# First stage of a long convolution on quarters of TensorE's array: even and odd positions apart, their sums and differences by VectorE and GpSimd

## The chip, the cores and the metric

One core of a Trainium2 chip runs the whole kernel. The metric is the device time of one execution in microseconds; the median of the runs shown counts. The engines are TensorE (PE; its weight loads are shown as PEld), VectorE (DVE), ScalarE (ACT), GpSimd (POOL) and SyncE (SP), which issues the DMAs here. TensorE multiplies a stationary operand by a moving one into PSUM; the other engines work between PSUM and SBUF, except that GpSimd works in SBUF alone.

## What is computed

The input is x, 8 sequences of 6400 positions and 128 channels in fp32, and a filter h of 6400 positions and 128 channels. Each channel is convolved with its filter (causally, by Fourier transforms), and then goes through a gated projection:

```python
Yf = np.fft.rfft(x, n=2*S, axis=1) * np.fft.rfft(h, n=2*S, axis=0)[None]
y = np.fft.irfft(Yf, n=2*S, axis=1)[:, :S, :]
gate = sigmoid(sum(conv_w[k] * shifted(y, 4 - k) for k in range(5)))
out = (gate * (y @ w_val)) @ w_out
```

## The kernel before

**The transform.** A sequence of 6400 positions is seen as 100 x 64. For each channel the transform is made in four stages, all matmuls in fp32:

- First stage (`first_stage`): over the 100. The stationary operand is one channel's 100 x 64 block of x, the moving one 100 columns of the constant `r1_sb` (cosines, or minus the sines), so that the real part lands in PSUM's partitions 0 to 63 and the imaginary part in 64 to 127. A group is 8 channels, 16 matmuls in the code, and fills a place of two PSUM banks. It is then copied into `gy` (the filter's into `dt`) by two copies of 400 elements a partition, both by ScalarE or both by VectorE (`ev`). A sequence has 16 groups.
- Second stage (`second`, 13 blocks of 8 of the 100 frequencies): over the 64, with the constant m2 from memory as stationary operand; then the product with the filter's spectrum (`product`: three long VectorE operations, a copy by ScalarE or GpSimd) and a sum (`summed`) by GpSimd, or for the last MANY blocks by either GpSimd or VectorE; the very last always by VectorE.
- Third stage (`third`): over the 64 back, in two pieces of 512 columns a block, copied out and stored to memory (`zd`).
- Fourth stage (in `longconv_moe`, "chunk"): read back from `zd`, over the 100 back; then five taps for the gate (ScalarE, VectorE, and for tap 3 GpSimd's addition of what ScalarE scaled), the sigmoid, the two projections, the multiplication and the store (`gated`).

**Halves of the array.** Every product of the kernel uses 64 columns of the stationary operand at a time, and two such halves work side by side on different output partitions (`product_of`; in the first stage the real and the imaginary part). In the profile a matmul of the code is two MATMUL and two LDWEIGHTS records, and the 64 columns stand as "*64" in the shape.

**The order.** Nothing is ordered by hand. `_Plan` takes every step with its costs on the engines that may do it (`_pe`, `_act`, `_dve`, `_pool`, `_dma`: formulas in ns written in the code), its predecessors, its PSUM place and its buffers. `due` gives each step a due time from the constants at the top of the file (HEADS, PERIOD, FIRST, SECOND, FOURTH, GATE and so on), `forward` plays the run through and gives each free engine the ready step that is due first. The resulting order is written into the program, and each engine then works through its queue in that order. The fourth stage of one sequence is so woven into the first and second stage of the next.

**Buffers.** PSUM has two places of two banks for the first and second stage (a third one only until the fourth stage begins) and places of one bank for the others. Groups of x are loaded (256 KB each) into buffers that come free when the group's matmuls are done; in steady state there are four. Thirteen buffers k serve the second and third stage. GpSimd steps marked `port` wait, by an added dependency, for the last VectorE step that is marked so.

**Where the profile puts it.** Every operation goes through one helper, so nearly all rows carry L124; the tiles tell them apart. First stage: `ps<-r_sb,x` (or `m_sb`, `y_all`, where the first loads of x lie in buffers that are free at the start). Second: `ps<-gy`. Third: `pb<-k,r_sb`. Fourth: `pb<-m_sb,dt`. Projections: `pb<-y_all,w_sb` and `pb<-dt,w_sb`.

The diff touches lines 31 to 73 (constants), `_constants` (85), `_Op` (163), `_Plan.forward` (236), `longconv_moe` (409) with `first_stage` (551), and `_lay_x` (998).

Of the kernel before, what the change touches and what calls it, by code (L numbers as in the profile page):

```python
# [30 lines left out]
CHUNKS = [HEAD] + [(a, CH) for a in range(0, 60, CH)]  # L31
NCH = len(CHUNKS)
OUT_ORDER = CHUNKS[1:] + [HEAD]
SECOND_END = 44851
FOURTH_END = 7729
GATE_END = 16494
EARLY_END = 14954
QTAPS = (3,)
LAST_QTAPS = (3,)
QB = 2  # L40
# [4 lines left out]
SLOTS = 13  # L45
SPARE = 2
RING = 4
MANY = 2
XB = 4
YB = 6  # L50
HEADS = 46300
HEAD_STEP = 5159
HEAD_END = 112668
PERIOD = 108461
WEIGHTS = 26000
M4 = 60000
ROWS = 50000
FIRST = 1583
SECOND_AT = 44851
SECOND = 4057  # L60
EARLY = 14954
FOURTH = 7729
GATE = 16494
PATIENCE = 380
ROUSE = 3
LASTQ = 10
FIRST3 = 0
LAST3 = 1
SWAPPED = ()
LAST = 3444  # L70
LAST_GATE = 12987
LAST_EARLY = 9555
LAST_LAG = 10


def _out_range(ch):
# [8 lines left out]
def _constants():  # L85
    k1 = np.arange(N1, dtype=np.float64)
    n1 = np.arange(N1, dtype=np.float64)
    k2 = np.arange(N2, dtype=np.float64)
    n2 = np.arange(N2, dtype=np.float64)
    tau = 2.0 * np.pi  # L90
    a = tau * np.outer(n1, k1 + 0.25) / N1
    r1 = np.concatenate([np.cos(a), -np.sin(a)], axis=1)
    al = tau * (
        (k1[None, :, None] + 0.25) * n2[:, None, None] / N
        + np.outer(n2, k2)[:, None, :] / N2
    )
    m2 = np.zeros((2, N2, N1, 2 * N2))
    m2[0, :, :, :N2] = np.cos(al)
    m2[1, :, :, :N2] = np.sin(al)
    m2[0, :, :, N2:] = -np.sin(al)  # L100
    m2[1, :, :, N2:] = np.cos(al)
    b = tau * np.outer(k2, n2) / N2
    r3 = np.zeros((2 * N2, N2, 2))
    r3[:N2, :, 0] = np.cos(b)
    r3[N2:, :, 0] = -np.sin(b)
    r3[:N2, :, 1] = -np.sin(b)
    r3[N2:, :, 1] = -np.cos(b)
    t = N2 * n1[None, :] + n2[:, None]
    g = tau * (k1[:, None, None] + 0.25) * t[None] / N
    m4 = np.zeros((PX, N2 + 1, N1))  # L110
    m4[:N1] = np.concatenate([np.cos(g), np.sin(g[:, :1])], axis=1) / N
    f = lambda v: np.ascontiguousarray(v.astype(np.float32))
    return f(r1), f(m2.reshape(2 * N2, N1, 2 * N2)), f(r3.reshape(2 * N2, 2 * N2)), f(m4.reshape(PX, -1))
# [45 lines left out]
class _Op:  # L159
# [3 lines left out]
    def __init__(self, run, cost, after, bank=None, new=False, port=False, take=None, use=(), wait=(), spare=0):  # L163
        self.run, self.cost, self.bank, self.new, self.port = run, cost, bank, new, port
        self.take, self.use, self.wait, self.spare = take, list(use), [*use, *wait], spare
        for s in [*self.use, *([take] if take else [])]:
            s.users.append(self)
        self.after = [a for a in after if a is not None]
        self.rank = self.at = self.done = self.engine = None


class _Plan:
# [63 lines left out]
    def forward(self):  # L236
# [3 lines left out]
        halves = [[0] * 2 for _ in range(4)]  # L240
        slots = [0] * SLOTS
        self.split = False
        port = server = now = 0
        events, began, lanes = [], [], []
        for o in self.ops:
            o.at = None
# [12 lines left out]
        def fits(o, e):  # L259
            if o.port and e == "vector" and port > now + self.PATIENCE:  # L260
                return False
            if any(max(free[x], now) + c[1] < now + o.cost[e][1] for x, c in o.cost.items() if x != e):
                return False
            if any(s.spot is None for s in o.wait) or o.take is not None and len(open_slots(o)) <= o.spare:
                return False
            b = o.bank
            if b is None:
                return True
            if o.new:
                return all(x.spot is not None for x in b.before) and self.room(b, halves, now) is not None  # L270
            return not any(x != e and t > now for x, t in b.seen)
# [5 lines left out]
        while left:  # L277
            moved = True
            while moved:
                moved = False  # L280
                for e in free:
                    if free[e] > now:
                        continue
                    kept, o = [], None
                    while ready[e]:
                        item = heapq.heappop(ready[e])
                        if item[2].at is not None:
                            continue
                        if fits(item[2], e):
                            o = item[2]  # L290
                            break
                        kept.append(item)
                    for item in kept:
                        heapq.heappush(ready[e], item)
                    if o is None:
                        continue
                    occ, dur = o.cost[e][:2]
                    if o.port and e in ("vector", "gpsimd") and port > now:
                        occ, dur = occ + port - now, dur + port - now
                    o.engine, o.at = e, now  # L300
                    free[e] = now + occ
                    if e == "sync":
                        server = max(now + self.LEAD, server) + dur
                        free[e] = max(free[e], server - self.LEAD - self.AHEAD)
                        o.done = server + self.LAND
                        lanes.append(o.done)
                        free[e] = max(free[e], *lanes[-8:-7], 0)
                    else:
                        o.done = now + dur + self.HOP
                    if o.port and e in ("vector", "gpsimd"):  # L310
                        port = now + dur
                    if o.take is not None:
                        i = o.take.spot = min(open_slots(o), key=lambda i: slots[i])
                        slots[i] = None
                    for s in [*o.use, *([o.take] if o.take else [])]:
                        s.left -= 1
                        if not s.left:
                            slots[s.spot] = max(u.done for u in s.users)
                            heapq.heappush(events, (slots[s.spot], -1, None))
                    b = o.bank  # L320
                    if b is not None:
                        if o.new:
                            i, h = b.spot = self.room(b, halves, now)
                            self.split = self.split or i == 2 and b.n == 1
                            for k in (0, 1) if b.n == 2 or i < 2 else (h,):
                                halves[i][k] = None
                        b.seen.append((e, now + dur + self.HOP))
                        b.left -= 1
                        if not b.left:
                            i, h = b.spot  # L330
                            for k in (0, 1) if b.n == 2 or i < 2 else (h,):
                                halves[i][k] = max(u.done for u in b.users)
                                heapq.heappush(events, (halves[i][k], -1, None))
                    began.append(o)
                    left -= 1
                    heapq.heappush(events, (o.done, self.index[id(o)], o))
                    heapq.heappush(events, (free[e], -1, None))
                    heapq.heappush(events, (now + dur, -1, None))
                    heapq.heappush(events, (now + dur + self.HOP, -1, None))
                    moved = True  # L340
# [68 lines left out]
def longconv_moe(ctx: ExitStack, tc: tile.TileContext, x, h, r1, m2, r3, m4, w64, out):  # L409
# [11 lines left out]
    ga = dt[:, : N2 * N1].rearrange("p (n t) -> p n t", t=N1)  # L421
    z_t = [dt[:, N2 * N1 + i * 2 * CH * C :][:, : 2 * CH * C] for i in range(RING)]
    m4_sb = cp.tile([PX, N2 + 1, N1], F32, name="m4_sb")
    r1_sb = cp.tile([N1, 2 * N1], F32, name="r1_sb")
    r3_sb = cp.tile([128, 2 * N2], F32, name="r3_sb")
    w_sb = cp.tile([C, NW], F32, name="w_sb")
    wc_sb = w_sb[:, 2 * C :]
# [103 lines left out]
    add(rouse, {"tensor": _pe(860, ROUSE)}, [zero], bank=warm, new=True)  # L531
    plan.base = -1500
    loads, firsts, x_at, x_last = [], [], [], {}
    r1_in = dma(r1_sb, r1, 80)
    spare = [m4_sb.rearrange("k n t -> k (n t)")[:, i * XG * N2 : (i + 1) * XG * N2] for i in range(8)]
    spare += y_sb
    x_more = x_sb + [i.rearrange("k (g n) -> k g n", n=N2) for i in spare]
# [1 line left out]
    def load(src):  # L539
# [8 lines left out]
        x_last[i] = n  # L548
        x_at.append(x_more[i])

    def first_stage(src, dst, before, base, step, groups=range(NG)):
        done = []
        for g in groups:
# [3 lines left out]
            load(src[g])  # L557
            t, bank = x_at[n], _Bank(2)

            def mm(e, t=t, bank=bank):  # L560
                for j in range(XG):
                    for c in range(2):
                        nc.tensor.matmul(
                            bank.ap()[c * N2 : (c + 1) * N2, j // 4, (j % 4) * N1 : (j % 4 + 1) * N1],
                            lhsT=t[:N1, j, :],
                            rhs=r1_sb[:, c * N1 : (c + 1) * N1],
                            start=True,
                            stop=True,
# [429 lines left out]
def _lay_x(v):  # L998
    b = v.shape[0]
    q = np.zeros((b, PX, C, N2), np.float32)  # L1000
    q[:, :N1] = v.reshape(b, N1, N2, C).transpose(0, 1, 3, 2)
    q = q.reshape(b, PX, NG, XG, N2).transpose(0, 2, 1, 3, 4)
    return np.ascontiguousarray(q)


def _lay_out(v):
# [33 lines left out]
```

## Time and profile before

| | |
|---|---|
| median of 3 runs | 965.06 us (962.79 to 965.62) |
| the profiled execution | 962.3 us |
| its span | 960.5 us |
| granted TensorE clock | 0.999 |
| TensorE busy | 942.0 us, 98% |
| VectorE busy | 703.7 us, 73% |
| ScalarE busy | 606.5 us, 63% |
| GpSimd busy | 362.7 us, 38% |
| moved by DMA | 283.27 MB, mean 295 GB/s |

All times in the rows below are of the one profiled execution. A row of a group has, after the shapes and the count, the group's busy time in us, the mean of one in ns, and the idle time of the engine ahead of it with what ended it. A row in order of time has the start in us, the length in us, the engine, the operation and the count of records that were merged; its length includes the modelled end of the last matmul. A row of a tile has the shortest, median and longest duration in ns, and the first and last start. The slice of each row of stretches begins with its start and end in us from the beginning of the span.

### The profile page before, as it was taken

To read this page: it belongs to the slowest core of one execution; us is meant where nothing else is said; L and a number is where in the kernel's file an instruction comes from. 1 tells how busy PE (TensorE), PEld (TensorE's weight loads), DVE (VectorE), ACT (ScalarE), POOL (GpSimd) and SP (SyncE) were. 2 spreads that over 40 slices of the span, in tenths; PEclk is the share of its full clock that TensorE was granted. 3 is DMA by queue.
4 is the path that set the end of the run, shared out by engine and by line. 5 is a ranking of instruction groups with operands and counts; after the bars stand their busy time and mean duration, and the time that the engine had idled before them with its cause. 6 is when DMAs were issued, how large, how long until landed. Compare 5 with 4: busy or idle time off the path is not lost.

```text
span 960.5 us, 32555 instructions
## 1 busy us (share of the span) xinstructions
PE 942.0 (98%) x13956; PEld 701.9 (73%) x13956; DVE 703.7 (73%) x855; ACT 606.5 (63%) x1053; POOL 362.7 (38%) x233
## 2 busy tenths in 40 slices
PE   9899999999999999999999999999999999999897
PEld 8888897667966689666876679766886669765553
DVE  2047718996399946998399964999379973999497
ACT  5665666566675657756566666756576666756664
POOL 0045503761047412554046611574026630465230
PEclk9999999999999999999999999999999999999999
DMA  9999798989979997999979898899979999695762
GB/s 349 355 344 323 262 368 284 311 272 342 340 226 325 289 369 263 287 285 329 363 237 320 278 344 320 245 308 309 361 255 297 280 334 333 203 328 180 263 212 105
DMA packets 183902, 283.27 MB, mean 295 GB/s; under 512 B 10538, under 2 KB 128654, under 8 KB 183694
## 3 DMA queue, kind: packets, MB, share of 16 engines
q1 hardware_dynamic: 183758, 281.19, 87.5%
q8 instruction: 110, 1.80, 0.7%
q14 instruction: 34, 0.28, 0.1%
HBM read 195.95 MB, written 88.92 MB: 297 GB/s over the span
## 4 chain that ended last, share of the span: by engine, by line
PE 92%; DVE 5%; issue 2%; POOL 1%; DMA 1%; ACT 0%; DVEq 0%; POOLq 0%
PE pb L124 49%; PE ps L124 43%; DVE dt L124 3%; DVE k L124 1%; POOL dt L124 1%; DMA dt<-zd 1%; ACT dt L124 0%; ACT k L124 0%; ACT q L124 0%; ACT y_head L124 0%; DVE q L124 0%; DVEq L124 0%; POOLq L124 0%
## 5 line engine op out<-in xcount | busy, mean ns | idle before, releaser
L124 DVE SCALAR_TENSOR_TENSOR dt<-pb,w_sb,dt 128x500 f32<-128x500 f32 (+7 forms) x328 | 221.6, 686 | 92.1 <-ACT y_head L124 56.1
L124 POOL TENSOR_TENSOR dt<-dt,q 128x500 f32<-128x500 f32 x93 | 116.6, 1253 | 371.5 <-DVE dt L124 285.8
L124 DVE TENSOR_TENSOR k<-ps,k 64x1024 f32<-64x1024 f32 (+2 forms) x208 | 244.3, 1177 | 5.9 <-issue 3.6
L124 POOL TENSOR_TENSOR k<-k,k 128x1024 f32<-128x1024 f32 x89 | 210.8, 2379 | 93.3 <-DVE k L124 89.8
L124 PEld LDWEIGHTS pb<-m_sb,dt 100*64 100x64 f32 x3976 | 179.5, 137 | 38.4 <-issue 17.4
L124 PE MATMUL pb<-k,r_sb 128*64 128x512 f32 x800 | 192.6, 594 | 0.7 <-DVE dt L124 0.7
L124 PEld LDWEIGHTS ps<-r_sb,x 100*64 100x64 f32 x3776 | 171.0, 137 | 27.1 <-issue 24.5
L124 PE MATMUL pb<-m_sb,dt 100*64 100x100 f32 x3976 | 186.6, 249 | 0.3 <-DVE k L124 0.3
L124 ACT COPY k<-pb 128x512 f32<-128x512 f32 (+1 forms) x207 | 119.0, 580 | 99.6 <-PE pb L124 65.6
L124 PE MATMUL ps<-r_sb,x 100*64 100x100 f32 x3776 | 175.6, 250 | 2.7 <-issue 2.7
L124 ACT COPY gy<-ps 128x400 f32<-128x400 f32 x242 | 114.4, 531 | 79.3 <-PE ps L124 79.3
L124 DVE SCALAR_TENSOR_TENSOR k<-ps,k 64x1024 f32<-64x1024 f32 (+1 forms) x104 | 123.2, 1185 | 55.0 <-PE ps L124 48.7
L124 PEld LDWEIGHTS ps<-gy,k 128*64 128x64 f32 x2176 | 129.3, 135 | 35.9 <-issue 21.3
L124 ACT COPY y_all<-pb 128x500 f32<-128x500 f32 x156 | 89.4, 579 | 93.4 <-PE pb L124 90.5
L124 PE MATMUL ps<-gy,k 128*64 128x128 f32 x2176 | 139.6, 278 | 0.4 <-issue 0.2
L124 PEld LDWEIGHTS pb<-k,r_sb 128*64 128x64 f32 x800 | 56.8, 136 | 80.7 <-issue 52.6
L124 PE MATMUL pb<-dt,w_sb 128*64 128x500 f32 (+2 forms) x412 | 102.4, 574 | 7.0 <-DVE dt L124 6.8
L124 ACT COPY k<-k 64x1024 f32<-64x1024 f32 (+1 forms) x78 | 81.1, 1040 | 17.4 <-DVE k L124 16.2
L124 DVE TENSOR_TENSOR dt<-pb,dt 128x500 f32<-128x500 f32 (+2 forms) x102 | 67.3, 660 | 29.7 <-PE pb L124 16.9
L124 PE MATMUL pb<-y_all,w_sb 128*64 128x500 f32 x336 | 85.1, 588 | 0.0
L124 POOL COPY k<-k 64x1024 f32<-64x1024 f32 (+1 forms) x39 | 36.8, 945 | 104.7 <-ACT k L124 64.9
L124 ACT ACTIVATE dt<-pb,w_sb 128x500 f32<-128x500 f32 (+1 forms) x107 | 68.8, 650 | 7.6 <-PE pb L124 7.5
(53 smaller groups left out, 575.3 us busy)
## 6 DMA issues: line engine op xcount, KB each, us to landing
dt<-zd SPq DMA_DIRECT2D x95, 640.0 KB, 5.6
zd<-k SPq DMA_DIRECT2D x96, 512.0 KB, 4.7
k<-hd SPq DMA_DIRECT2D x84, 512.0 KB, 5.7
k<-m SPq DMA_DIRECT2D x64, 512.0 KB, 5.6
x<-xl SPq DMA_DIRECT2D x110, 256.0 KB, 5.4
out<-y_all SPq DMA_DIRECT2D x84, 250.0 KB, 4.6
hd<-k SPq DMA_DIRECT2D x12, 512.0 KB, 4.5
dt<-zd SPq DMA_DIRECT2D x8, 512.0 KB, 6.6
```

Source lines behind the costliest of these rows:

```text
L124: r = self._tc.keep_in_program_order(call(*args, **kwargs))
```

## The change

From the second sequence on (`QUARTERS = 32` groups: 16 of the filter and 16 of the first sequence stay on the old path) the first stage uses a symmetry of the transform: with the 100 positions split into even and odd ones, frequency k and frequency k + 50 are the sum and the difference of the same two products. So the 50 even positions lie in partitions 0 to 49 and the 50 odd ones in 64 to 113, both in x and in `r1_sb`, and a group is made of 32 matmuls in the code: 50 rows by 64 columns, with 50 moving columns, for each of 8 channels, 2 row halves and 2 column halves. The even products go to one PSUM bank and the odd ones to the other. ScalarE copies both banks (800 elements) to a k buffer, VectorE adds the odd part's copy to the even part in PSUM and writes frequencies 0 to 49 of `gy`, and GpSimd or VectorE writes frequencies 50 to 99 as the difference of the two copies. The filter and the first sequence keep the full contraction, over 128 partitions, in which the new gaps are zeros.

The plan learns of the two shapes: a step has a mode, a change of mode is booked at 95 ns, and while TensorE is in quarters, ready quarter steps that are due within 2175 ns go first. Nearly all due-time constants are new, and MANY goes from 2 to 1 (only the last block's sum is VectorE's). PAIRED is 0, so the lines that it guards do nothing; HALF is 50; BRISK and SLOW are not used.

```diff
-SECOND_END = 44851
-FOURTH_END = 7729
-GATE_END = 16494
-EARLY_END = 14954
+SECOND_END = 42124
+FOURTH_END = 7349
+GATE_END = 16413
+EARLY_END = 13447
...
-MANY = 2
+MANY = 1
...
-HEADS = 46300
-HEAD_STEP = 5159
-HEAD_END = 112668
-PERIOD = 108461
+HEADS = 42326
+HEAD_STEP = 5131
+HEAD_END = 108957
+PERIOD = 101559
...
-FIRST = 1583
-SECOND_AT = 44851
-SECOND = 4057
-EARLY = 14954
-FOURTH = 7729
-GATE = 16494
+FIRST = 2231
+SECOND_AT = 42124
+SECOND = 3721
+EARLY = 13447
+FOURTH = 7349
+GATE = 16413
...
-LAST = 3444
-LAST_GATE = 12987
-LAST_EARLY = 9555
+LAST = 3223
+LAST_GATE = 13546
+LAST_EARLY = 10558
 LAST_LAG = 10
+HALF = 50
+SWITCH = 95
+SAME = 2175
+QUARTERS = 32
...
-    r1 = np.concatenate([np.cos(a), -np.sin(a)], axis=1)
+    w = np.concatenate([np.cos(a), -np.sin(a)], axis=1)
+    r1 = np.zeros((PX, 2 * N1))
+    r1[:HALF], r1[N2 : N2 + HALF] = w[::2], w[1::2]
...
-                    while ready[e]:
+                    if e == "tensor" and mode:
+                        same = [x for x in ready[e] if x[2].mode and x[2].at is None and x[0] < now + SAME and fits(x[2], e)]
+                        if same:
+                            o = min(same)[2]
+                    while ready[e] and o is None:
...
+                    if e == "tensor" and o.mode != mode:
+                        occ, dur, mode = occ + SWITCH, dur + SWITCH, o.mode
...
+    def quarters(g, t, bank, loaded, dst, old):
+        def mm(e, t=t, bank=bank):
+            for j in range(XG):
+                for r in range(2):
+                    for c in range(2):
+                        rows = slice(r * N2, r * N2 + HALF)
+                        nc.tensor.matmul(
+                            bank.ap()[c * N2 : (c + 1) * N2, r, j * HALF : (j + 1) * HALF],
+                            lhsT=t[rows, j, :],
+                            rhs=r1_sb[rows, c * N1 : c * N1 + HALF],
+                            start=True,
+                            stop=True,
+                        )
+        p = add(mm, {"tensor": _pe(118, 8)}, [loaded, r1_in], bank=bank, new=True)
+        p.mode = 1
...
+        kept_ = _Slot()
+        half = lambda v: v.rearrange("p (m t k) -> p m t k", t=2, k=HALF)
+        both = lambda s=kept_: s.ap()[:, : 2 * XG * HALF].rearrange("p (r x) -> p r x", r=2)
+        to = lambda r, g=g: dst(g)[:, :, r * HALF : (r + 1) * HALF].rearrange("p m k t -> p m t k")
+        def out_(e, bank=bank, both=both):
+            nc.scalar.copy(both(), bank.ap()[:, :, : XG * HALF])
+        def plus(e, bank=bank, both=both, to=to, half=half):
+            nc.vector.tensor_tensor(out=to(0), in0=half(bank.ap()[:, 0, : XG * HALF]), in1=half(both()[:, 1]), op=ADD)
+        def minus(e, both=both, to=to, half=half):
+            getattr(nc, e).tensor_tensor(out=to(1), in0=half(both()[:, 0]), in1=half(both()[:, 1]), op=ALU.subtract)
+        o = add(out_, {"scalar": _act(800)}, [p], bank=bank, take=kept_)
+        x = add(plus, {"vector": _dve(400)}, [o, *old], bank=bank, use=[kept_])
+        y = add(minus, {"gpsimd": _pool(400), "vector": _dve(400)}, [o, *old], port=True, use=[kept_])
+        return [x, y]
...
+            if n >= QUARTERS:
+                done += quarters(g, t, bank, loads[n], dst, before(g))
+                continue
...
-                            lhsT=t[:N1, j, :],
+                            lhsT=t[:, j],
...
-    q[:, :N1] = v.reshape(b, N1, N2, C).transpose(0, 1, 3, 2)
+    u = v.reshape(b, N1, N2, C).transpose(0, 1, 3, 2)
+    q[:, :HALF], q[:, N2 : N2 + HALF] = u[:, ::2], u[:, 1::2]
```

More of the change, by code (lines that the diff above doesn't have):

```diff
@@ L69 @@
 SWAPPED = ()
-LAST = 3444
-LAST_GATE = 12987
-LAST_EARLY = 9555
+LAST = 3223
+LAST_GATE = 13546
+LAST_EARLY = 10558
 LAST_LAG = 10
+HALF = 50
+SWITCH = 95
+SAME = 2175
+QUARTERS = 32
+BRISK = 9
+SLOW = 12000
+PAIRED = 0
 def _out_range(ch):
@@ L168, in __init__ @@
         self.after = [a for a in after if a is not None]
-        self.rank = self.at = self.done = self.engine = None
+        self.rank = self.at = self.done = self.engine = self.partner = None
+        self.mode = 0
 class _Plan:
@@ L242, in forward @@
         self.split = False
-        port = server = now = 0
+        port = server = now = mode = 0
         events, began, lanes = [], [], []
@@ L268, in fits @@
                 return True
+            if PAIRED and o.mode and not mode and o.partner is not None and o.partner.at is None:
+                if need[id(o.partner)] or sum(all(t is not None and t <= now for t in p) for p in halves[:3]) < 2:
+                    return False
             if o.new:
@@ L423, in longconv_moe @@
     m4_sb = cp.tile([PX, N2 + 1, N1], F32, name="m4_sb")
-    r1_sb = cp.tile([N1, 2 * N1], F32, name="r1_sb")
+    r1_sb = cp.tile([PX, 2 * N1], F32, name="r1_sb")
     r3_sb = cp.tile([128, 2 * N2], F32, name="r3_sb")
@@ L533, in longconv_moe @@
     loads, firsts, x_at, x_last = [], [], [], {}
-    r1_in = dma(r1_sb, r1, 80)
+    r1_in = dma(r1_sb, r1, 100)
     spare = [m4_sb.rearrange("k n t -> k (n t)")[:, i * XG * N2 : (i + 1) * XG * N2] for i in range(8)]
@@ L549, in load @@
         x_at.append(x_more[i])
+    def quarters(g, t, bank, loaded, dst, old):
[13 more added lines that the diff above has]
+        p.mode = 1
+        p.partner = firsts[-1] if g % 2 else None
+        if g % 2:
+            firsts[-1].partner = p
+        firsts.append(p)
+        kept_ = _Slot()
[12 more added lines that the diff above has]
+        return [x, y]
     def first_stage(src, dst, before, base, step, groups=range(NG)):
@@ L1000, in _lay_x @@
     q = np.zeros((b, PX, C, N2), np.float32)
-    q[:, :N1] = v.reshape(b, N1, N2, C).transpose(0, 1, 3, 2)
-    q = q.reshape(b, PX, NG, XG, N2).transpose(0, 2, 1, 3, 4)
-    return np.ascontiguousarray(q)
+    u = v.reshape(b, N1, N2, C).transpose(0, 1, 3, 2)
+    q[:, :HALF], q[:, N2 : N2 + HALF] = u[:, ::2], u[:, 1::2]
+    return np.ascontiguousarray(q.reshape(b, PX, NG, XG, N2).transpose(0, 2, 1, 3, 4))
 def _lay_out(v):
```

## The prediction

> **What bounds the kernel now.** I read the page first (busy shares and the chain that ended last), then a table of busy time by stretch over one steady sequence, then the matmuls in order of time, and last the durations by form.
>
> ```profile
> span 960.5 us, 32555 instructions
> ...
> PE 942.0 (98%) x13956; PEld 701.9 (73%) x13956; DVE 703.7 (73%) x855; ACT 606.5 (63%) x1053; POOL 362.7 (38%) x233
> ...
> PE 92%; DVE 5%; issue 2%; POOL 1%; DMA 1%; ACT 0%; DVEq 0%; POOLq 0%
> ```
>
> TensorE is busy 98% of the span and makes up 92% of the chain, so TensorE work is worth its full length if nothing else comes up beside it. What could come up is VectorE; the table by stretch says where it has room (columns: length, busy time of PE, PEld, DVE, ACT, POOL with instruction counts, clock, DMA share, GB/s).
>
> ```profile
> 326.00:332.00 6.00, 6.00 (x74) 3.82 (x72) 5.89 (x7) 4.37 (x8) 2.07 (x3) 1.00 1.05 373
> 332.00:338.00 6.00, 6.00 (x70) 3.36 (x68) 5.51 (x10) 4.70 (x9) 1.26 (x1) 1.00 0.95 289
> 338.00:344.00 6.00, 6.00 (x114) 4.92 (x112) 4.04 (x6) 3.75 (x9) 1.56 (x2) 1.00 1.07 358
> 344.00:350.00 6.00, 6.00 (x114) 4.92 (x112) 2.41 (x4) 3.14 (x8) 0.99 (x2) 1.00 1.02 356
> 350.00:356.00 6.00, 6.00 (x104) 4.57 (x100) 1.36 (x2) 3.00 (x7) 0.00 (x0) 1.00 1.03 406
> 356.00:362.00 6.00, 6.00 (x134) 5.63 (x132) 1.15 (x2) 3.17 (x7) 0.00 (x0) 1.00 1.02 355
> 362.00:368.00 6.00, 6.00 (x146) 6.00 (x144) 1.80 (x6) 4.63 (x10) 0.00 (x0) 1.00 0.98 344
> 368.00:374.00 6.00, 6.00 (x126) 5.47 (x124) 4.30 (x7) 5.64 (x12) 1.25 (x1) 1.00 0.92 307
> 374.00:380.00 6.00, 6.00 (x98) 4.96 (x95) 5.46 (x8) 3.62 (x6) 1.25 (x1) 1.00 0.55 176
> 380.00:407.00 27.00, 26.97 (x364) 18.95 (x362) 25.79 (x28) 19.00 (x31) 16.67 (x9) 1.00 0.84 265
> 407.00:434.00 27.00, 27.00 (x312) 17.15 (x310) 26.03 (x27) 15.52 (x27) 16.49 (x10) 1.00 0.92 295
> sum 108.00, PE 107.97 PEld 79.76 DVE 83.76 ACT 70.55 POOL 41.54; mean PE 9.82 PEld 7.25 DVE 7.61 ACT 6.41 POOL 3.78
> ```
>
> TensorE has no idle time in this sequence. VectorE is nearly full from 380 on (second and third stage), and idle for most of 338 to 374: busy 4.04+2.41+1.36+1.15+1.80+4.30 = 15.1 of 36 us. That stretch is where the first-stage groups lie:
>
> ```profile
> 333.36 1.55 PE L124 MATMUL ps<-r_sb,x 100*64 100x100 f32 x32
> ...
> 359.14 5.67 PE L124 MATMUL ps<-r_sb,x 100*64 100x100 f32 x128
> 364.63 3.62 PE L124 MATMUL pb<-m_sb,dt 100*64 100x100 f32 x80
> 368.06 2.93 PE L124 MATMUL ps<-r_sb,x 100*64 100x100 f32 x64
> ```
>
> The 16 groups of a sequence (32 recorded matmuls each, two for every one in the code) come in nine runs; the first and the last two are shown, the whole list being runs of 1, 1, 3, 2, 1, 1, 1, 4 and 2 groups. Four groups take from 359.14 to 364.63, so one takes **1.372 us**: 16 pairs of load and matmul for each half of the columns, one every 85.8 ns.
>
> **Part 1, the quarters: a gain.** A group becomes 64 recorded pairs of half the length, 16 for each of four quarters. Seven sequences times 16 groups, 112, are changed. No row shows quarters working side by side, so I bound the price of a group.
>
> ```profile
> L124 PE MATMUL ps<-r_sb,m_sb x640: 246/249/300, 10.5 to 53.3; 100*64 100x100 f32 x160
> L124 PEld LDWEIGHTS ps<-r_sb,m_sb x640: 132/137/137, 10.5 to 53.2; 100*64 100x64 f32 x160
> 901.86 0.20 PEld L124 LDWEIGHTS pb<-dt,w_sb 128*64 128x64 f32 x4 [2.20 <-DVE dt L124]
> 350.53 0.15 PEld L124 LDWEIGHTS pb<-dt,w_sb 128*64 128x64 f32 x2
> ```
>
> Floor by streaming: half of 85.8 is 43 ns a pair, 16 pairs, 0.69 us. Ceiling: the two row halves take turns and nothing is won, 1.372 us. Between them stands the weight load, which doesn't shrink with the rows or the moving columns: 64 columns as now. The longest matmul of this form lasts 300 ns where the median is 249; the excess of 51 ns is the one that began on an empty array and had to wait for its own load. And on restart at 901.86 four loads (two per half) take 0.20 us, so the second two begin up to 0.20 - 0.136 = 64 ns behind, less the 7 to 14 ns between the halves (0.15 - 0.136 in the last row): 50 to 57 ns. A load thus holds a quarter 51 to 57 ns, more than the 43 that it streams. I take 57, the row's upper end: 16 x 57 = **0.91 us**, a gain of 0.46 us a group, 112 x 0.46 = **-51.5 us**, provided that four quarters load at once as two halves do now. At 51 ns it is -62.3. The new plan itself books 944 ns for a group; that is an assumption in the diff, not a measurement.
>
> **Part 2, changing over: a loss.** Everything else stays on 128x64 halves, so each run of quarters has a border on either side. No row shows such a border. At least the first load can't be prefetched under the last matmul: 51 ns. At most the array must run empty as well: a matmul of 249 ns streams for 86, so its tail is 163 (its end is modelled), 163 + 51 = 214 ns. I take **0.11 us**, nearer to the lower end because the tail is the modelled part. The Trainium skill ("TensorEngine Tiling (Array Packing)", Key Properties) speaks against the change here: a change of tiling mode drains TensorE. By that rule the upper figure of 214 ns is the price, and the sum would be 13 us higher. No run shown here has a change of mode.
>
> How many: nine runs now. The new order prefers quarters while in quarters, which makes runs longer; but two PSUM places of two banks hold it to about two groups at a time. I keep nine: 18 borders x 0.11 = 2.0 us a sequence, x 7 = **+13.9 us**. Ends: 6.4 (51 ns) and 27.0 (214 ns); 24.6 if all 16 groups stand alone at 0.11.
>
> **Part 3, the evacuation: mostly hidden.**
>
> ```profile
> L124 ACT COPY gy<-ps 128x400 f32<-128x400 f32 x242 | 114.4, 531 | 79.3 <-PE ps L124 79.3
> L124 ACT COPY k<-ps 128x1024 f32<-128x1024 f32 x12 | 12.2, 1013 | 18.0 <-PE ps L124 18.0
> L124 ACT COPY k<-pb 128x512 f32<-128x512 f32 x188 | 108.6, 583 | 91.2 <-PE pb L124 57.3 <-issue 23.2 <-POOL k L124 9.2
> L124 DVE TENSOR_TENSOR dt<-pb,dt 128x400 f32<-128x400 f32 x8 | 4.6, 574 | 9.0 <-PE pb L124 9.0
> L124 DVE TENSOR_TENSOR k<-k,k 128x1024 f32<-128x1024 f32 x7 | 8.5, 1215 | 0.0
> L124 POOL TENSOR_TENSOR k<-k,k 128x1024 f32<-128x1024 f32 x89 | 210.8, 2379 | 93.3 <-DVE k L124 89.8 <-DMA k<-m 3.2
> L124 POOL TENSOR_TENSOR dt<-dt,q 128x500 f32<-128x500 f32 x93 | 116.6, 1253 | 371.5 <-DVE dt L124 285.8 <-ACT q L124 47.3 <-DVE k L124 34.8
> 345.10 1.06 DVE L124 COPY gy<-ps 128x400 f32<-128x400 f32 x2 [1.55 <-PE ps L124]
> ```
>
> ScalarE: two copies of 400 (0.53 each) become one of 800: 583 + 288 x 430/512 = 825 ns; 16 x 0.825 against 30 x 0.531 a sequence is 2.7 us less. VectorE gets a sum of 400 from PSUM per group: 16 x 0.574 = 9.2 us a sequence, less the two copies that it does now (1.1) and one of the last long sums, which the smaller MANY sends to GpSimd (1.2): **+6.9**. GpSimd gets the differences, at 1253 - 100 x 1126/524 = 1.04 us, and that sum: 16 x 1.04 + 2.4 = +19 on 41.5. If all differences went to VectorE, another 16 x 0.574 = 9.2 there. Of the 24.2 us in which VectorE idles, 6.9 go to the new work and about 5 to the shorter sequence: 12 are left, mainly beside the first stage, where the sums fall due. So I cost the volume at nothing, and if that cover were gone, at 6.9 us a sequence.
>
> The chain is another matter. The sum waits for ScalarE's copy, and behind it on VectorE's queue stand the previous sequence's taps, which the gates wait for. GpSimd's difference waits for the same copy and, by the port rule, for a VectorE operation; behind it stand GpSimd's additions of tap 3, which the sigmoid needs. A place stays taken for 0.83 + 0.57 = 1.40 us behind the matmuls, where two copies hold it 0.95 to 1.06 now. With two places, a run of more than two groups moves at (0.91 + 0.2 + 1.40)/2 = 1.26 us a group rather than 0.91. In today's runs three groups of 16 are the third or fourth: 3 x 0.35 x 7 = 7 us at most; other stages' matmuls fill most of that. I take **+3**, between 0 and 8.
>
> **Part 4, what moves.** All due times are reset, and with them the places of the 16 loads of x (256 KB each) on SP's queue, past the loads of m2 and the spectrum and the stores of the last output. The bytes don't change apart from 28 rows of r1. At 304 GB/s a sequence (the stretches' mean), a sequence 5 us shorter needs 320, and stretches of 355 to 406 stand above: nothing. The copy takes one of the 13 k buffers, in a stretch where GpSimd and VectorE leave them idle: nothing. In the last sequence no first stage runs:
>
> ```profile
> 866.00:960.00 94.00, 81.07 (x962) 48.34 (x960) 72.44 (x107) 56.24 (x100) 26.01 (x20) 0.99 0.56 189
> ```
>
> Its 13 us without TensorE stay, with new due times for 0, give or take 4.
>
> **Sum.** Against the profiled execution: 962.3 (span 960.5 and 1.8 around it) - 51.5 + 13.9 + 3 = 927.7. The median shown is 965.06, 2.8 above, so I forecast **930.5 us**.
>
> **The rivals.**
> *Slower: pairs begin no faster than today's burst.* Four loads within 64 ns are one per 21.3 ns, and today's steady rate is 1.372/32 = 42.9. If TensorE can't begin pairs faster than 21.3 whichever quarter they go to, a group takes 64 x 21.3 = 1.36 us, the gain falls to 1 us in all, and the borders remain: 962.3 - 1 + 13.9 + 2.8 = **978**. It decides from (1.372 - 0.124)/64 = 19.5 ns a pair. The same time comes out if the row halves take turns. Against it: the two loads of 350.53 begin 14 ns apart. For it: no row shows a steady rate anywhere near 14. Chance 0.08, taken over every such floor. The Trainium skill ("TensorE: Matmul & The Clock Gate", Part 1) has a floor of this kind: matmul starts are never closer than about 25 ns. By it a group would take 1.60 us and the kernel some 1004; of the 0.08 it has 0.03. The 14 ns of the trace disagree with that floor for a pair on two halves; a long series isn't shown.
> *No change: the evacuation paces every group.* All 112 at 1.26 us: 112 x 0.11 = 12.3 won, 13.9 lost: **967**. Against it: ScalarE waits for TensorE 79.3 us before these copies, so it is early now, and only three groups in 16 stand deep in a run. Chance 0.05. Where half of the groups are so paced: about 947, inside my range.
> *More: borders nearly free.* At 51 ns and with no loss at the banks: 962.3 - 51.5 + 6.4 + 2.8 = 920; with loads of 51 ns too, 909. Together **914**, chance 0.12.
> That the change doesn't do what it says is excluded: the counter reaches 32 behind h and the first sequence, so all 112 groups take the new path.
>
> **How the numbers follow.** My forecast has 0.75. Its own range is 917 (loads of 51 ns) to 949 (borders of 214 ns and 8 us at the banks: 962.3 - 51.5 + 27 + 8 + 2.8). The range reaches down to 913 to take in half of the better case. A measurement here tells 0.3%, about 3 us, from no change. Faster: 0.75 + 0.12 = 0.87; same 0.05; slower 0.08.
>
> **What would show it.** Matmuls of the form 50x50 on r_sb and x, 64 a group; four groups' starts or one group's first to last start give the 0.91; a gap ahead of the first and behind the last gives the border; the clock stays at 1.00. VectorE should rise to about 90 us a sequence and GpSimd to 60. Wrong I would be if a group takes over 1.2 us, if borders cost over 0.2, or if TensorE shows idle time behind VectorE's sums in mid-sequence.

## The result, and the profile after

| | before | after |
|---|---|---|
| median | 964.87 us (4 runs, 962.79 to 965.62) | 1067.67 us (4 runs, 1058.57 to 1072.6) |
| span of the profiled execution | 960.5 us | 1068.3 us |
| granted TensorE clock | 0.999 | 0.939 |

The changed kernel is slower: ratio 1.106, 95% interval 1.098 to 1.114. The forecast was 930.5 us, with a range to 949, and a chance of 0.08 for slower.

The page of the changed kernel, in the rows that answer to those of before (span, busy shares, clock in tenths over 40 slices, chain):

```profile
span 1068.3 us, 39959 instructions
...
PE 973.3 (91%) x17540; PEld 700.3 (66%) x17540; DVE 760.8 (71%) x978; ACT 592.7 (55%) x951; POOL 468.2 (44%) x324
...
PEclk9999959999889998999899998999969998799999
...
PE 82%; issue 9%; DVE 7%; ACT 1%; DMA 1%; POOL 0%; DVEq 0%; ACTq 0%; POOLq 0%
```

TensorE is now idle for 9% of the span, and "issue", time in which an engine waits for nothing that the profile shows, has grown from 2 to 9% of the chain. The clock row has slices from 5 to 8 where it was all nines. Two stretches of one sequence show where (columns as in the table of stretches of before):

```profile
367.00:427.00 60.00, 50.87 (x1390) 38.70 (x1388) 29.81 (x53) 32.97 (x52) 19.02 (x19) 0.89 0.82 267
427.00:487.00 60.00, 58.42 (x674) 36.95 (x672) 58.87 (x61) 33.62 (x54) 36.36 (x21) 1.00 0.83 264
```

Only the stretch with the first stage suffers: TensorE idles for 9 of 60 us, at a mean clock of 0.89, while VectorE is half idle. There TensorE's matmuls read, in order of time:

```profile
367.38 2.08 PE L133 MATMUL ps<-r_sb,x 50*64 50x50 f32 x128
369.40 1.06 PE L133 MATMUL pb<-dt,w_sb 128*64 128x500 f32 x4
...
381.88 1.84 PE L133 MATMUL ps<-r_sb,x 50*64 50x50 f32 x108
385.42 0.55 PE L133 MATMUL ps<-r_sb,x 50*64 50x50 f32 x20 [1.70 <-issue]
385.90 1.75 PE L133 MATMUL pb<-dt,w_sb 128*64 128x500 f32 x4
```

The first row is what was forecast: two groups (128 matmuls) in 2 us. The third row breaks off after 108 of 128 matmuls, in the middle of a group whose inputs are all there, for 1.70 us. And behind a stop the clock falls: the matmuls of 385.90 (four of 500 columns) take 1.75 us, where the same four at 369.40 take 1.06. The sums of these stops, by tile, from the waits:

```profile
PE ps L133 <- issue: 54.7, 29, 3.9
PE pb L133 <- issue: 13.0, 9, 4.8
```

38 stops of over 0.2 us, 67.7 us in all; before it were 4 with 3.4 us. They have one thing in common, which no view shows but which can be counted from the records. If TensorE's records (loads, matmuls and its semaphore waits) are numbered in order of start, the first one behind each stop has the number

```
193 or 194 modulo 256   38 of 38 stops (changed kernel)
193 modulo 256           4 of  4 stops (kernel before, at 26.95, 44.49, 50.73 and 151.62)
```

So TensorE stops at the borders of blocks of 256 instructions. The queue that brings instructions (q8 of the page) moves blocks of 16,384 bytes, and each stop ends 1.2 to 1.6 us behind the landing of one:

```profile
q8 instruction: 138, 2.26, 0.8%
```

138 blocks, where the kernel before had 110; 35,441 records of TensorE in 138 blocks are 257 a block. From the record 256 places earlier to the first one behind a stop it took 3.3 to 7.3 us, median 5.5. I call that the round of a block: at these 38 stops TensorE got 256 records in it and no more. It has three parts in the trace: 0.7 to 4.9 us (median 3.2) until the transfer of the block begins, 1.0 us of transfer (median), and the 1.2 to 1.6 us from the landing to the first record. A group of quarters has 128 records (64 loads and 64 matmuls), and two groups take 1.87 us where nothing stops them.

### The profile page after: what moved, and what is told of

The parts are those of the page before. It is cut to its first block, busy times and chain, and to the rows that moved or that the text cites. A ratio compares the mean times of both kernels' runs of the same rounds, so it can differ in the third digit from the quotient of the medians.

```text
span 1068.3 us, 39959 instructions
## 1 busy us (share of the span) xinstructions
PE 973.3 (91%) x17540; PEld 700.3 (66%) x17540; DVE 760.8 (71%) x978; ACT 592.7 (55%) x951; POOL 468.2 (44%) x324
## 4 chain that ended last, share of the span: by engine, by line
PE 82%; issue 9%; DVE 7%; ACT 1%; DMA 1%; POOL 0%; DVEq 0%; ACTq 0%; POOLq 0%
PE pb L133 46%; PE ps L133 36%; DVE k L133 3%; DVE dt L133 3%; ACT k L133 1%; DMA dt<-zd 1%; ACT dt L133 0%; POOL dt L133 0%; POOL k L133 0%; DVE y_all L133 0%; DVE gy L133 0%; ACT y_head L133 0%; DVEq L133 0%; DVE q L133 0%; ACTq L133 0%
## 5 line engine op out<-in xcount | busy, mean ns | idle before, releaser
L133 POOL TENSOR_TENSOR k<-k,k 128x1024 f32<-128x1024 f32 x96 | 227.6, 2378 | 124.6 <-DVE k L133 67.0
L133 DVE SCALAR_TENSOR_TENSOR dt<-pb,w_sb,dt 128x500 f32<-128x500 f32 (+7 forms) x328 | 221.6, 685 | 42.9 <-POOL dt L133 27.0
L133 PEld LDWEIGHTS pb<-m_sb,dt 100*64 100x64 f32 x3976 | 199.1, 150 | 45.0 <-issue 22.9
L133 PE MATMUL pb<-m_sb,dt 100*64 100x100 f32 x3976 | 212.9, 268 | 12.2 <-issue 12.2
L133 PE MATMUL ps<-r_sb,x 50*64 50x50 f32 (+1 forms) x7168 | 151.7, 236 | 52.9 <-issue 51.2
L133 PEld LDWEIGHTS ps<-r_sb,x 50*64 50x64 f32 (+1 forms) x7168 | 140.8, 149 | 80.6 <-issue 70.1
L133 POOL TENSOR_TENSOR gy<-k 128x400 f32<-128x400 f32 x81 | 84.0, 1043 | 233.1 <-ACT k L133 223.0
L133 ACT COPY k<-ps 128x800 f32<-128x800 f32 (+3 forms) x129 | 107.5, 834 | 126.8 <-PE ps L133 113.8
L133 DVE TENSOR_TENSOR gy<-ps,k 128x400 f32<-128x400 f32 x112 | 64.2, 573 | 154.6 <-ACT k L133 154.3
L133 ACT COPY k<-pb 128x512 f32<-128x512 f32 (+2 forms) x197 | 114.6, 582 | 80.6 <-PE pb L133 74.4
L133 PEld LDWEIGHTS ps<-gy,k 128*64 128x64 f32 x2176 | 135.4, 140 | 29.5 <-issue 24.8
```

Of the source, the lines that this page charges most:

```text
L133: r = self._tc.keep_in_program_order(call(*args, **kwargs))
```

## The experiments

I set up three theories. **Supply:** TensorE's instructions come too slowly for quarters, and the idle time lowers the clock. **Gate:** the clock is lowered because quarters count as little work. **Order or evacuation:** the new due times, or the sums and differences, hold TensorE up. Each of these runs was a single one beside a run of the kernel before on the same chip (967.15 us for the first four, 963.43 for the next three, 964.99 for the last two).

**Half the matmuls, still in quarters**

```diff
-                    for c in range(2):
-                            bank.ap()[c * N2 : (c + 1) * N2, r, j * HALF : (j + 1) * HALF],
+                    c, i = j % 2, j // 2
+                            bank.ap()[c * N2 : (c + 1) * N2, r, i * N1 : (i + 1) * N1],
...
-                            rhs=r1_sb[rows, c * N1 : c * N1 + HALF],
+                            rhs=r1_sb[rows].rearrange("p (c k) -> p c k", c=2)[:, :, :HALF],
```

> The changed kernel with its order, its evacuation and its quarters, but the quarters take 100 moving columns (50 cosines and 50 sines) for one channel, and the two column halves take two different channels: 16 matmuls in the code a group where the changed kernel has 32, and fewer records (32) than the old form's 32. Real and imaginary parts land in other places, so what is computed from them is left out of the claim; all sizes are the same. Supply theory (TensorE's instructions come in blocks of 16 KB, a block about every 3.7 us at best, and quarters use them up faster; the idle time then lowers the clock): the stalls put down to issue fall from 68 us to under 10, the clock goes back to 0.99 or more, a group takes 0.69 us, and the time is 962 - 112 x 0.68 + 14 for the borders + 3 = 903, at most 920. Gate theory (the clock is lowered because quarters count as little work, stalls or not): the clock stays at 0.95 or less, and the time stays above 950. Evacuation theory (sums and differences hold TensorE up): the time stays above 1000 with waits for VectorE and ScalarE.

Measured: 960.41 us, clock 0.986, 18 stops by issue with 20.3 us.

```profile
PE 902.4 (94%) x13956; PEld 628.0 (66%) x13956; DVE 759.8 (79%) x978; ACT 586.7 (61%) x951; POOL 467.8 (49%) x324
```

```profile
334.99 1.60 PE L133 MATMUL ps<-r_sb,x 50*64 50x100 f32 x64
336.53 1.06 PE L133 MATMUL pb<-dt,w_sb 128*64 128x500 f32 x4
```

The quarters, the order, the evacuation and the data are those of the changed kernel; the number of records is down to that of before, each matmul has 100 columns instead of 50, and 107 us are gone. By the two traces that is about 47 us of stops, 44 of clock and 28 of work (0.69 us a group for 0.94), less 8 us of other idle time that came on top. Two groups take 1.54 us with the border behind them (334.99 to 336.53). That speaks for supply and against evacuation. Of the gate theory the time came (above 950) and the clock (0.95 or less) did not. The supply theory's own figures were missed as well: instead of 903 us, 17 us of stops remain beyond those of before, 20 us of other idle time (29.1 for 9.5), and 12 us by a lower clock.

**The new order alone**

```diff
-QUARTERS = 32
+QUARTERS = 10**9
```

> The changed kernel's constants and layout with the old first stage for all sequences (no quarters). Supply and gate theory: no new stalls, clock 1.00, 955 to 980 us. Order theory (the new due times are what costs): above 1000 us.

Measured: 970.67 us, clock 1.000, 5 stops by issue (3.3 us). The order costs 3.5 us in this pair of runs, less than the spread of the kernel before (962.79 to 967.15). Order theory falls.

**The double number of records, without quarters**

```diff
-                    for c in range(2):
+                    for k in range(2 if n >= 32 else 1):
+                        for c in range(2):
+                            w = N1 // 2 if n >= 32 else N1
...
-                            rhs=r1_sb[:, c * N1 : (c + 1) * N1],
+                                rhs=r1_sb[:, c * N1 + k * w : c * N1 + (k + 1) * w],
```

> The kernel before, where in the seven later sequences each first-stage matmul is cut in two of 50 moving columns, on the halves of the array as before: the doubled instruction count of the change without its quarters. The work alone, by a weight load of 55 ns: 32 x 55 = 1.76 us a group, 112 x 0.39 = 44 us more, 1006 us. Supply theory: 256 instructions in 3.5 us is about the rate at which blocks come, so there are some stalls by issue in the first stage (10 to 40 us), and the time lies between 1010 and 1050. Gate theory: no stalls, clock 1.00, 1006 us, give or take 5.

Measured: 1052.25 us, clock 0.979, 15 stops by issue (16.2 us). All 15 end at 193 or 194 modulo 256.

```profile
129.78 3.78 PE L124 MATMUL ps<-r_sb,y_all 100*64 100x50 f32 x123
135.92 9.32 PE L124 MATMUL ps<-r_sb,y_all 100*64 100x50 f32 x171 [2.35 <-issue]
```

The kernel before, on halves of the array and in its own order, gets the same kind of stop and the same half clock as soon as its records are doubled: around the stop the clock goes to half and stays there for 30.7 us. A group takes 1.85 us here (1.76 expected): 112 x 0.48 = 54 us, with 13 of stops and 21 of clock 88, where 85 was measured. The time is 2 us above the range of the supply theory. So quarters aren't needed for either effect.

**Less data beside it: small loads, and light DMA**

```diff
-        loads.append(dma(x_more[i], src, 256,
+        part = slice(0, 1) if n >= 2 * NG + 10 else slice(0, XG)
+        loads.append(dma(x_more[i][:, part], src[:, part], 256,
```

> The changed kernel, where the loads of x from the middle of the second sequence on bring 1 channel of 8 (32 KB, not 256 KB); the rest of the buffer keeps old data, so the output is of no meaning. It takes some 100 GB/s out of the stretch of the first stage. Supply theory with blocks queueing behind data: the stalls by issue fall to a half or less, and the time falls by 40 us or more. Supply theory with a fixed round of fetching: stalls, clock and time as in the changed kernel, within 15 us. Gate theory: the clock stays as low, the time within 15 us.

Measured: 1053.76 us, clock 0.944, 35 stops with 53.5 us: 14 us of stops less, at an unchanged median round of 5.5 us. Queueing behind data was to bring 34 us of stops and 40 us of time, and that did not come. The time lies 13.9 us below the changed kernel's median, within the 15 us that the fixed round and the gate theory allowed; but the changed kernel itself ranges over 14 us (1058.57 to 1072.6), so this single run decides little. The second run took the fourth stage's loads down as well:

```diff
-                zt[:PX, : 2 * n * C], zd[b % 2][:, 2 * a * C : 2 * (a + n) * C],
+                zt[:PX, : n * C // 4], zd[b % 2][:, 2 * a * C : 2 * a * C + n * C // 4],
```

> The changed kernel with far less data moved beside the first stage: the loads of x as in the run with small loads (1 channel of 8), and the fourth stage's loads from memory cut to an eighth of their columns (the rest of each buffer keeps old data, so the output is of no meaning). Every stall by issue of the changed kernel ended at a record whose number is 193 or 194 modulo 256, at a median of 5.5 us (3.3 to 7.3) after the one 256 records before. Supply theory, blocks queueing behind data: this round falls towards the shortest one seen, 3.3 to 4 us, the stalls fall from 68 us to under 30, and the time to 1010 or less. Supply theory with a round that doesn't depend on the traffic: 45 us of stalls or more, above 1035. Gate theory: clock 0.95 or less whatever the stalls do.

Measured: 1018.17 us, clock 0.955, 25 stops with 28.9 us, at a median round of 4.4 us (5.5 in the changed kernel): the stops as expected of queueing, the time 8 us above it. The part of the round that shrank is the wait until a block's transfer begins (median 2.1 us for 3.2); the transfer itself took 1.0 us in both. So a part of the round gets shorter with less data beside it, which fits waiting behind data; stops remain even so. The clock stayed at 0.955, just above the bound of the gate theory (0.95 or less); that left the clock open.

**Quarters for one group in four**

```diff
-            if n >= QUARTERS:
+            if n >= QUARTERS and n % 4 == 0:
```

> The changed kernel with quarters for one group in four (28 of 112), the other groups in the old form. In work: 28 x (1.372 - 0.94) = 12 us less, and 28 x 0.233 = 6.5 us for the borders, measured in the changed kernel as 0.10 us ahead of a run and 0.13 behind it; against the run of the order alone (970.7) that is 965. Supply theory: a block of 256 records then holds 128 of a quarter group and as many at the old rate, 0.94 + 2.75 = 3.7 us against a round of 5.5, so single stalls of 1 to 2 us remain at some of the 28, 15 to 30 us with what the clock loses: 975 to 1000. Gate theory (quarters themselves lower the clock): a group of 0.94 us is a quarter of a window, the clock stays at 0.99 or more, and the time is 965.

Measured: 980.58 us, clock 1.000, 14 stops by issue with 13.1 us.

```profile
374.40 2.67 PE L133 MATMUL ps<-r_sb,x 50*64 50x50 f32 x96
376.90 1.54 PE L133 MATMUL pb<-m_sb,dt 100*64 100x100 f32 x32
379.54 0.56 PE L133 MATMUL pb<-m_sb,dt 100*64 100x100 f32 x8 [1.08 <-issue]
```

The clock stays up with 28 groups of quarters; the stops are still there, short and single, and even this dose is 10 us slower than the order alone (the kernels before beside them took 963.43 and 967.15). The row at 379.54 shows that the bill needn't come where it is made: the stop falls into the fourth stage's matmuls, 2 us behind the quarters.

**What the clock follows.** The low stretches of all runs begin and end on a grid of 3.41 us and are multiples of it, at a clock of 0.5. I worked out, for every window of that grid, the share of the array and of the time (at the clock of that window) in which operands streamed, counting a quarter as a quarter:

```
window is followed by a fall to 0.5      share 0.46 or less (changed kernel, 15 windows), 0.47 or less (seven other runs)
window at 0.5, followed by full clock    share 0.63 or more, in most cases over 0.85
windows at 0.5 that stay there           up to 0.95
```

These shares are estimates, since the trace has the starts of matmuls and only models their ends; how a matmul is laid over the border of two windows moves a share by up to 0.1. Every fall came behind a window with less than about half of streaming (some such windows, between 0.3 and 0.4, brought none), and full clock came back only behind a well filled window, though not behind each. Quarters come in twice. Their stops make empty windows, and when dense they stream for only 43 of each 59 ns, 0.73, with low stretches of up to 27.3 us. The kernel with the doubled records on halves did no better at 50 columns (30.7 us). With 100 moving columns the run with half the matmuls was back after two windows at most; but the full kernels below, with 100 columns too and more idle time between them, had low stretches of 20.5, 17.1 and 10.2 us. So that 50 columns as such hold the clock down is not shown. Whether dense quarters would hold the full clock if no stop came wasn't tried, since the stops can't be taken away without changing the number of matmuls.

**A full kernel on half the matmuls.** The paired form needs real and imaginary parts put back in place. ScalarE did it with four copies of 64 partitions:

```diff
-            nc.scalar.copy(both(), bank.ap()[:, :, : XG * HALF])
+            for h in range(2):
+                for c in range(2):
+                    v = both()[c * N2 : (c + 1) * N2].rearrange("p r (m t k) -> p r m t k", t=2, k=HALF)[:, :, :, h]
+                    i = bank.ap()[h * N2 : (h + 1) * N2, :, : XG * HALF]
+                    nc.scalar.copy(v, i.rearrange("p r (m c k) -> p r m c k", c=2, k=HALF)[:, :, :, c])
```

> A full kernel on the half count of matmuls: 100 moving columns, the two column halves take two channels, and ScalarE puts real and imaginary parts back in place with four copies of 64 partitions (about 1.9 us a group for 0.83), sums and differences from the copies by VectorE and GpSimd; due times as in the changed kernel. Supply theory: stalls by issue near the 20 us of the run with the half count, clock 0.98 or more; ScalarE has 112 x 1.1 = 120 us more to do, its copies hold a place of PSUM 0.6 us longer, and the due times aren't made for it: 965 to 1000. Evacuation theory: waits for ScalarE's copies dominate, above 1000.

Measured: 1032.09 us, clock 0.955, but only 5 stops by issue (7.0 us); 81.3 us of idle time by other causes. Here the evacuation theory is right, for a kernel with another evacuation: about half of that idle time (41 us) ends with ScalarE's copies, most of the rest (34 us) with VectorE's work for the fourth stage (tile dt). And it speaks on the clock: that is as low as in the run with light DMA, with hardly a stop by issue, so a low clock comes with idle time of other causes too.

Then the order was made for it. The plan got the block as a resource:

```diff
+                        def late(x):
+                            occ, _, k = x.cost[e]
+                            into = spent + k - BLOCK
+                            return max(0, block - now - occ * (k - into) / k) if k and into >= 0 else 0
```

with BLOCK 256 and a round of 5.8 us, and an operation that would run into a block's end early was put behind others.

> The full kernel on the half count of matmuls again, with an order made for it: the plan now books 256 records of TensorE per 5.8 us (an operation that would run into the end of a block too early is put back behind others), books ScalarE's four copies, and its due times were searched anew. Supply theory: stalls by issue under 20 us, clock 0.99 or more, waits for ScalarE below the 81 us of other idle time of the first such kernel, and 940 to 975. Evacuation theory: the four copies still hold TensorE up, over 990.

> The same, with each of the four copies free to go to ScalarE or VectorE, and due times searched for that. Supply theory: as in the run before it or 5 to 15 us faster, 935 to 970. Evacuation theory: within 5 us of the run before it, over 990, since the chain of four copies remains.

Measured: 986.82 us (6 stops, 6.1 us; clock 0.984; other idle time 59.0 us) and 974.51 us (9 stops, 5.7 us; clock 0.983; 47.2 us). The stops are gone, down to the level of the kernel before, but both miss the expected times, by 12 and by 5 us, and the clock of 0.99. The largest share of the idle time that is left (22 of 47 us in the second run) ends with ScalarE's copies:

```profile
470.89 1.67 PE L135 MATMUL ps<-r_sb,x 50*64 50x100 f32 x64
474.06 0.92 PE L135 MATMUL ps<-r_sb,x 50*64 50x100 f32 x32 [1.50 <-ACT k L135]
```

Two groups fill both places of PSUM, and the third waits for ScalarE's copies, six of which run from 472.00 to 475.03. No version of the whole computation that was run beats the kernel before.

## Why the prediction was wrong, point by point

**The step that failed** is in Part 1, "the quarters: a gain". From "TensorE has no idle time in this sequence" (true: 107.97 of 108.00 us) it was concluded that TensorE's work sets the pace, and a group was priced by what the array does with it, streaming and weight load. Nothing was asked of where its instructions come from: the sum has no term for stops by issue, which cost 64 us, and none for the clock, which cost 55. The records doubled from 64 to 128 a group. In the kernel before, 64 in 1.372 us are 46.6 a microsecond, 256 in 5.5 us, about the median round of a block in the changed kernel (the four stops of the kernel before had rounds of 6.2 to 7.1 us): the first stage before stands close to what the supply gives. The quarters asked for 136.

**The prices of the work were right.** Two groups without a stop take 1.865 us from first to last start, 127 steps of 14.7 ns: 0.94 us a group (0.91 forecast). The borders of 18 undisturbed runs cost 0.10 us ahead of the run and 0.13 behind it (0.11 forecast each), and the runs came in twos (48 of 50 runs, where the prediction had kept 63). TensorE gained 112 x 0.43 = 48 us and lost 50 x 0.23 = 12 at borders. On top came, between the two profiled executions:

```
quarters                         - 48
borders                          + 12
stops by issue (67.7 for 3.4)    + 64
other idle time (20.7 for 9.5)   + 11
half clock (112 us of work)      + 55
not attributed                   + 14
span                             +108
```

The half clock is 129 us long, 17 of them idle; half of the other 112 is lost, less 1 in the kernel before. The new order has no row of its own: its 3.5 us, measured by itself, came with 6 us more of other idle time in that run, which would be counted twice.

**The drain.** The Trainium skill's rule ("TensorEngine Tiling (Array Packing)", Key Properties), that a change of tiling mode drains TensorE, agrees in kind: a border costs 0.10 and 0.13 us. It was not the upper figure of 0.214.

**The evacuation** was priced well (827 ns a copy, 573 a sum, 1043 a difference; 825, 574 and 1040 forecast) and wasn't the cause, as the run with half the matmuls shows: it has the same evacuation.

**The slower rival** had the right place and the wrong reason. It said that pairs begin no faster than some pace whatever their quarter, named 42.9 ns as today's steady rate, and then took 21.3 from a burst of four. The burst is no measure: as long as a block lasts, any burst goes through. A round of 5.5 us gives 128 pairs, 43 ns a pair. That this equals today's 42.9 is chance: 42.9 is the array's pace with 100 columns, since in the run with half the matmuls each quarter takes a matmul every 86 ns as well, at twice the records a microsecond. At 43 ns a pair a group would take 64 x 43 = 2.75 us. Between most groups stand other stages with fewer records; the longest run of quarters in the changed kernel, 12 groups from 128.52 to 155.40, took 2.24 us a group, with most of it at half clock, 1.5 us of it a wait for VectorE, and stops by issue at three borders. The floor of 25 ns between starts that the Trainium skill states ("TensorE: Matmul & The Clock Gate", Part 1) is not borne out: 128 starts came 14.7 ns apart.

**The clock** was written down as "stays at 1.00" without a reason; it was 0.939.

**What could have been seen.** The profile of before has a row of this kind

```profile
26.95 0.39 PE L124 MATMUL ps<-r_sb,x 100*64 100x100 f32 x4 [1.48 <-issue]
```

three times in its head (26.95, 44.49 and 50.73), where first-stage groups stand back to back: stops with nothing to wait for, in the very operation that was to be doubled. The Trainium skill ("Runtime: NRT & Kernel Launch", Instruction fetch mechanics) states that instructions come in blocks of 16 KiB, 256 instructions. The stops, at one and the same place in each count of 256, agree. It also says that the fetch is hidden by the pace of issue. The runs disagree: 67.7 us weren't hidden, and one block in 5.5 us is slower than the array.

## What to carry to other kernels

Before a matmul is cut into smaller ones, count the instructions of the stretch and set them against the pace at which the kernel before already issues there; a stretch without visible waits may stand at the limit of its supply, and idle rows put down to "issue" in its densest part say so. A gain on TensorE is then worth having only in a form that doesn't raise the count, and none of the full kernels that were tried in such a form beat the kernel before. Where the array falls idle in pieces of 1 to 4 us, the clock can add to the loss: 55 us beside 75 us of added idle time in the changed kernel, none beside the 13 us of stops in the run with quarters for one group in four.

## What the runs showed of the hardware that was not expected

- TensorE's instructions arrive in blocks of 256. Of 174 stops by issue in eleven runs, 173 ended at 193 or 194 modulo 256 and one at 195. The round of a block lay between 3.0 and 8.2 us, with medians from 4.4 (little data beside it) to 6.5 us.
- The clock falls to half for windows of 3.41 us behind a window with less than about half of streaming (an estimate from the traces), and among dense 50-column matmuls, which stream for three quarters of the time, it stayed there for 27 to 31 us. What exactly brings it back is open.
- Four quarters do load and stream at once: 14.7 ns a pair over 128 pairs, 59 ns a pair in each quarter; with the same 50 columns a half takes a pair every 58 ns in the run with the doubled records (1.85 us for 32).
